# First routed rows loaded from another queue, the sigmoid table fetched earlier, and w_out's conversion one unit later

## The chip, the cores and the metric

The kernel runs on one core of a Trainium2 chip. The core has five engines with a queue of instructions each: TensorE (PE in the profile; its weight loads are PEld), VectorE (DVE), ScalarE (ACT), GpSimd (POOL) and SyncE (SP), which here only issues DMAs. Each engine works through its queue in order; semaphores hold it where it needs another's result. The metric is the device time of one execution in microseconds (us).

## The reference

Three stages follow each other: a decaying linear attention, a mixture of experts in which each token goes to one expert, and a gated dense layer. In all of them the tensors are float32.

```python
def _attn_ref(q, k, v):              # 4 batches, 8 heads, 768 steps, head dim 64
    for t in range(S):
        state = gamma * state + outer(k[:, :, t], v[:, :, t])
        y[:, :, t] = scale * q[:, :, t] @ state

def _moe_ref(x, modality_id, w_gate, modality_bias, w1, w2):   # 3072 tokens of 512, 8 experts, hidden 1024
    e_idx = np.argmax(x @ w_gate + modality_bias[modality_id], axis=1)
    for e in range(E):
        out[mask] = gate_w[mask, None] * (np.maximum(x[mask] @ w1[e], 0.0) @ w2[e])

def _moe2_ref(x, w_in, w_out):       # 512 -> 2048 -> 512, weights in float64
    h = x @ w_in
    g = h * (1.0 / (1.0 + np.exp(-1.702 * h)))
    return (g @ w_out).astype(np.float32)
```

## The kernel before

Products of float32 are computed as three matmuls of rounded halves: a value is split into a high half (`hi`, a cast on ScalarE) and a low half (`lo`, the difference, on VectorE), and hi*hi, hi*lo and lo*hi are summed in PSUM.

**Stages.** The attention writes its rows to `xd` in DRAM. The routed stage works through slots, each a block of up to 256 tokens of one expert (B), or a tiny one of 32 (T). A slot gathers its rows (`xg`, an indirect DMA that GpSimd issues), transposes them, and runs units on PE: `b1` (first layer, 24 matmuls into `psh`), `second` (second layer, into `pso`), and for a tiny slot `th`, `tt` (a transpose `ptt` that VectorE copies to `htt`), `t2` (into `psq`, from `htt` and four weight tiles) and `ts`. Results go to `ys0` and `ys1` in DRAM; `ys0` holds the first two slots, which are finished early. Weights come through `raw` tiles loaded by SyncE and split by `split` into `whi` and `wlo`; a tiny slot loads its weights straight into such tiles.

**The last routed slot** has the units `b1`, `b1`, `th`, `second`, `tt`, `b1`, `t2`, `second`, `ts`, `b1`, `second`, `second`, the tiny slot's being laid between. After each of them one entry of the list `tail` (L1049) runs: `first_loads` (the first two blocks of 128 rows for the dense stage, tiles `yg`, read from `ys0`; both lie in the one buffer `xg`), two empty entries, `first_conv(0)` (loads of the next two pieces of `w_out`), `first_turn(0)`, `first_turn(1)` (which then issues the third load, again into buffer `xg`), two empty ones, `first_turn(2)`, `first_conv(1)`. `first_turn` calls `turn`: GpSimd copies the row numbers (`idd`), PE transposes four blocks (`pyt`), ScalarE and VectorE split the result to `yh` and `yl`.

**The dense stage** handles eight tiles of 384 tokens with 16 units each. In step i, `d1` makes twelve matmuls into `psd` (three PSUM buffers), the sigmoid on ScalarE, the product `g` on VectorE, and its halves `gh` and `gl`; then `d2` of the unit two steps back (LAG = 2) makes nine matmuls into `psq`: for each of three row blocks `gh` by `woh[f]`, `gh` by `wol[f]`, `gl` by `woh[f]`. So PE's order is psd(0), psd(1), psd(2), psq(0), psd(3), psq(1) and so on.

**w_out's conversion.** The weights come as float64 and are turned to float32 halves piece by piece (class `Conv`): the constructor loads a piece (SyncE, two buffers), `A` takes its magnitude and sign (ScalarE, L956 and L957), `B` assembles the bits (VectorE, L961 to L963), `C` is a step on ScalarE (L966) and GpSimd (L967), `E` casts `woh[f]` (ScalarE, L978) and `F` makes `wol[f]` (VectorE, L981). Unit 0's halves are made in the routed stage; pieces for units 1 to 15 are made in the first tile's steps, by `more_conv`, which `d1` calls between `g` and `gh`; `A` and `B` of the piece for unit 1 have been done by `first_conv(1)`.

```python
        p0, p1, p2 = at_(i + 1), at_(i), at_(i - 1)
        for p, fs in ((p1, "C"), (p0, "A"), (p2, "E"), (p0, "B"), (p2, "F")):
            if p:
                getattr(p, fs)()
```

Here `at_(k)` is the piece for unit k + 1. Between the two stages stands a conditional block (L1076) for slots that a rare routing would need; every engine reads its condition and branches past it. The order of every queue is the order in which the code is written.

Of the kernel before, what the change touches and what calls it, by code (L numbers as in the profile page):

```python
# [8 lines left out]
F32 = mybir.dt.float32  # L9
# [3 lines left out]
AF = mybir.ActivationFunctionType  # L13
# [9 lines left out]
C = 128  # L23
# [13 lines left out]
DW = DM + 1  # L37
RP1 = NP1 * BIG
T2 = 384
NF = DFF // C  # L40
# [53 lines left out]
def tile_kernel(ctx, tc, qn, kv, mod, wg, mbias, w1, w2, w_in, w_out, c_qc, c_misc, out):  # L94
    nc = tc.nc
# [14 lines left out]
    ident = M("id")  # L110
# [14 lines left out]
    mm = {}  # L125
# [808 lines left out]
    NE = 1  # L934
# [74 lines left out]
    outv = dram_disjoint_views(out, NT)  # L1009
    yt = [pool(ctx, "yt0", 1)]  # L1010

    def yload(t, r, y=None):
        n = t * NR + r
        if y is None:
            y = yp.tile([C, DW], F32, name="yg", tag="yg")
        src, n0 = (ys0, 0) if n < RP1 // C else (ys1, RP1 // C)
        nc.sync.dma_start(y, src[(n - n0) * C:(n - n0 + 1) * C, :])
        YG[t, r] = y

    def turn(t, r, ps):  # L1020
        if r == 0:
            YT[t] = [yt[t % 2].tile([C, 4, T2], F32R, name=f"y{x}", tag=f"y{x}") for x in "hl"]
        y = YG.pop((t, r))
        n = t * NR + r
        nc.gpsimd.tensor_copy(idd[:, n:n + 1], y.bitcast(I32)[:, DM:DW])
        for k in range(4):
            nc.tensor.transpose(ps[:, k, :], y[:, k * C:(k + 1) * C], ident)  # L1027
        yh, yl = (x[:, :, r * C:(r + 1) * C] for x in YT[t])
        nc.scalar.copy(yh, ps)
        V.tensor_tensor(out=yl, in0=ps, in1=yh.bitcast(F32), op=ALU.subtract)  # L1030

    def first_loads():
        y = mm["xg"].tile([C, 2, DW], F32, name="yg", tag="xg")
        for r in range(2):
            yload(0, r, y[:, r, :])

    def first_turn(r):
        turn(0, r, mm["t"].tile([C, 4, C], F32, name="pyt", tag="pt"))
        if r == 1:
            yload(0, 2, mm["xg"].tile([C, DW], F32, name="yg", tag="xg"))  # L1040

    cq = []

# [6 lines left out]

    none = lambda: None
    tail = [first_loads, none, none, lambda: first_conv(0), lambda: first_turn(0), lambda: first_turn(1), none, none, lambda: first_turn(2), lambda: first_conv(1)]
    fin = table_final()
    for _ in range(FIN_SLOTS - 1):
# [39 lines left out]
    def d1(t, f, mid=None):  # L1094
        yh, yl = YT[t]
        ps = ps_h.tile([C, T2], F32, name="psd", tag="psd")
        m = 0
        for k in range(4):
            for a, b in ((wih, yh), (wih, yl), (wil, yh)):
                nc.tensor.matmul(ps, a[:, k, f * C:(f + 1) * C], b[:, k, :], start=(m == 0), stop=(m == 11), skip_group_check=True)  # L1100
                m += 1
        sig = gg.tile([C, T2], F32, name="sig", tag="sig")
        nc.scalar.activation(sig, ps, AF.Sigmoid, scale=1.702)  # L1103
        g = gg.tile([C, T2], F32, name="g", tag="g")
        V.tensor_tensor(out=g, in0=ps, in1=sig, op=ALU.mult)  # L1105
        if mid:
            mid()
        gh = gt.tile([C, T2], F32R, name="gh", tag="gh")
        gl = gt.tile([C, T2], F32R, name="gl", tag="gl")
        nc.scalar.copy(gh, g)  # L1110
        V.tensor_tensor(out=gl, in0=g, in1=gh.bitcast(F32), op=ALU.subtract)  # L1111
        GT[t, f] = (gh, gl)

    def d2(t, fs):
        if fs[0] == 0:
            PO[t] = [ps_o.tile([C, DM], F32, name="psq", tag=f"psq{r}") for r in range(NR)]
        for r in range(NR):
            for f in fs:
                gh, gl = GT[t, f]
                for m, (a, b) in enumerate(((gh, woh), (gh, wol), (gl, woh))):  # L1120
                    nc.tensor.matmul(PO[t][r], a[:, r * C:(r + 1) * C], b[f], start=(f == 0 and m == 0), stop=(f == NF - 1 and m == 2), skip_group_check=True)  # L1121
            if f == NF - 1:
                o = ot.tile([C, DM], F32, name="o", tag="o")
                if r % 2:
                    V.tensor_copy(o, PO[t][r])  # L1125
                else:
                    nc.scalar.copy(o, PO[t][r])  # L1127
                n = t * NR + r
                nc.gpsimd.indirect_dma_start(out=outv[n], out_offset=bass.IndirectOffsetOnAxis(ap=idd[:, n:n + 1], axis=0), in_=o, in_offset=None)  # L1129
        for f in fs:  # L1130
            del GT[t, f]
        if f == NF - 1:
            del PO[t], YT[t]
# [3 lines left out]
    def more_conv(i):  # L1137
        if len(cq) < NF - NE:
            cq.append(Conv(NF + NE + len(cq)))
        at_ = lambda k: cq[k] if 0 <= k < NF - NE else None  # L1140
# [3 lines that stand above are left out]
                getattr(p, fs)()  # L1144

    for i, (t, f) in enumerate(seq):
        d1(t, f, lambda: more_conv(i) if i <= NF - NE else None)
        if t + 1 < NT2:
            if f in (5, 6, 7):
                yload(t + 1, f - 5)  # L1150
            elif f in (11, 12, 13):
                turn(t + 1, f - 11, ps_t.tile([C, 4, C], F32, name="pyt", tag="pyt"))
        if LAG <= i < len(seq):
            t, f = seq[i - LAG]
            d2(t, [f])
# [35 lines left out]
```

## Time and profile before

| | us |
|---|---|
| median of 3 runs | 999.86 |
| lowest and highest run | 993.59, 1003.96 |
| the profiled execution | 1001.46 |
| its span, first to last instruction | 999.8 |
| PE busy in it | 965.2 |
| DVE busy | 503.1 |
| ACT busy | 410.7 |
| POOL busy | 179.1 |
| mean granted clock of TensorE | 0.992 |

The profile comes from one execution. A row of a timeline is: start in us from the span's start, duration in us, engine, line of the code, operation, tile written <- tiles read, shapes, count, and in brackets the idle time of the engine just before, with what ended it. SPq and ACTq are an engine's own sequencer, which issues DMAs and branches. A row with a count over 1 merges neighbours and spans all of them. Matmuls overlap: one that takes 0.39 us is followed 0.23 us later by the next. A row of stretches gives the stretch, its length, the busy time (and count of instructions) of PE, PEld, DVE, ACT and POOL, the granted clock of TensorE as a share of 2.4 GHz, the mean share of the DMA engines and GB/s.

### The profile page before, as it was taken

The numbers are of one execution on the slowest core, as the hardware profiler recorded it, in microseconds if no ns is written. First come the engines' busy times: TensorE is split into PE (matmuls) and PEld (weight loads), VectorE is DVE, ScalarE is ACT, GpSimd is POOL, SyncE is SP. The second block draws the span as 40 slices with busy tenths as digits, with TensorE's granted clock in tenths as the row PEclk, the third lists the DMA queues.
The fourth block names the chain that finished last, engine by engine and source line by source line (L and its number), as shares of the span: only waits on it lengthen the run. The fifth ranks groups of instructions, "written<-read, shape, count | busy, mean of one in ns | idle before, by whom it ended". The sixth has DMA issues, their size and how long they took to land.

```text
span 999.8 us, 16732 instructions
## 1 busy us (share of the span) xinstructions
PE 965.2 (97%) x6610; PEld 855.2 (86%) x6610; DVE 503.1 (50%) x921; ACT 410.7 (41%) x728; POOL 179.1 (18%) x177
## 2 busy tenths in 40 slices
PE   8999879999999999999999999999999999999995
PEld 7888668899999987879999999998999998999994
DVE  3555568798888876449942322323323223223221
ACT  3433245576777665348732222222322223222221
POOL 2343334233322222003310010010100100100101
PEclk9999999999999999999999999999999999999998
DMA  8787689888888879925310100100001001000000
GB/s 288 225 217 199 126 217 227 265 271 285 284 266 270 282 242 333 324 67 177 127 43 1 33 32 1 33 32 22 27 17 32 32 1 33 32 1 1 32 1 31
DMA packets 43128, 128.18 MB, mean 128 GB/s; under 512 B 6976, under 2 KB 7360, under 8 KB 43040
## 3 DMA queue, kind: packets, MB, share of 16 engines
q1 hardware_dynamic: 34464, 107.96, 35.0%
q0 software_dynamic: 5120, 12.77, 3.7%
q10 hardware_dynamic: 3456, 6.29, 1.9%
q8 instruction: 53, 0.87, 0.4%
q14 instruction: 35, 0.29, 0.1%
HBM read 107.76 MB, written 19.24 MB: 127 GB/s over the span
## 4 chain that ended last, share of the span: by engine, by line
PE 54%; ACT 0%; DVE 0%; POOLq 0%; POOL 0%; issue 0%; ACTq 0%
PE psq L1121 27%; PE psd L1100 26%; PE pyt L1027 1%; ACT L1103 0%; POOLq L1187 0%; DVE ab L961 0%; DVE ab L963 0%; ACT o L1127 0%; ACT ab L956 0%; ACT ab L966 0%; ACT sig L1103 0%; DVE gl L1111 0%; DVE ab L962 0%; POOL out_dram L1129 0%; POOLq L1129 0%
## 5 line engine op out<-in xcount | busy, mean ns | idle before, releaser
L1105 DVE TENSOR_TENSOR g<-psd,sig 128x384 f32<-128x384 f32 x128 | 71.3, 557 | 279.7 <-ACT sig L1103 279.7
L1103 ACT ACTIVATE sig<-psd 128x384 f32<-128x384 f32 x128 | 62.9, 492 | 289.5 <-PE psd L1100 289.5
L1100 PE MATMUL psd<-yl,wih 128*128 128x384 f32 x512 | 172.1, 336 | 0.0
L1100 PE MATMUL psd<-yh,wil 128*128 128x384 f32 x512 | 171.9, 336 | 0.0
L1100 PE MATMUL psd<-yh,wih 128*128 128x384 f32 x512 | 171.6, 335 | 0.2 <-PEq L1076 0.2
L1121 PE MATMUL psq<-woh,gh 128*128 128x512 f32 x384 | 153.9, 401 | 0.7 <-ACT gh L1110 0.7
L1121 PE MATMUL psq<-woh,gl 128*128 128x512 f32 x384 | 152.2, 396 | 1.1 <-DVE gl L1111 1.1
L1121 PE MATMUL psq<-wol,gh 128*128 128x512 f32 x384 | 152.3, 397 | 0.0
L595 DVE TENSOR_TENSOR wlo<-raw,whi 128x1024 fp32r<-128x1024 f32 x93 | 113.4, 1224 | 32.6 <-ACT whi L593 29.3
L593 ACT CAST whi<-raw 128x1024 fp32r<-128x1024 f32 x96 | 99.9, 1046 | 42.0 <-issue 16.6
L689 PE MATMUL psh<-xh,whi 128*128 128x256 f32 x384 | 109.5, 285 | 0.2 <-ACT xh L676 0.2
L689 PE MATMUL psh<-xl,whi 128*128 128x256 f32 x384 | 107.9, 281 | 0.3 <-DVE xl L677 0.3
L689 PE MATMUL psh<-xh,wlo 128*128 128x256 f32 x384 | 107.7, 281 | 0.0
L1129 POOL DMA_INDIRECT out_dram<-o,idd x24 | 23.3, 973 | 462.5 <-DVE o L1125 387.5
L1111 DVE TENSOR_TENSOR gl<-g,gh 128x384 fp32r<-128x384 f32 x128 | 71.7, 560 | 65.0 <-ACT gh L1110 65.0
L1100 PEld LDWEIGHTS psd<-yh,wih 128*128 128x128 f32 x512 | 96.5, 188 | 6.3 <-PEq L1076 0.6
L1100 PEld LDWEIGHTS psd<-yl,wih 128*128 128x128 f32 x512 | 96.0, 188 | 5.8
L1100 PEld LDWEIGHTS psd<-yh,wil 128*128 128x128 f32 x512 | 96.1, 188 | 0.0
L1110 ACT CAST gh<-g 128x384 fp32r<-128x384 f32 x128 | 65.8, 514 | 70.3 <-DVE g L1105 70.2
L1121 PEld LDWEIGHTS psq<-woh,gl 128*128 128x128 f32 x384 | 72.1, 188 | 19.0 <-DVE gl L1111 1.5
L1121 PEld LDWEIGHTS psq<-woh,gh 128*128 128x128 f32 x384 | 72.0, 188 | 13.0 <-ACT gh L1110 1.0
L1121 PEld LDWEIGHTS psq<-wol,gh 128*128 128x128 f32 x384 | 72.3, 188 | 11.6
(195 smaller groups left out, 1516.4 us busy)
## 6 DMA issues: line engine op xcount, KB each, us to landing
raw<-in_w_dram SPq DMA_DIRECT2D x96, 512.0 KB
qk<-in_qn_dram SPq DMA_DIRECT2D x23, 512.0 KB
r<-in_w_in_dram SPq DMA_DIRECT2D x16, 512.0 KB
r<-in_w_out_dram SPq DMA_DIRECT2D x16, 512.0 KB
ys<-yo SPq DMA_DIRECT2D x12, 513.0 KB
yg<-ys SPq DMA_DIRECT2D x24, 256.5 KB
v<-in_kv_dram SPq DMA_DIRECT2D x24, 256.0 KB
xd<-xr ACTq DMA_DIRECT2D x24, 256.0 KB
```

Of the source, the lines that this page charges most:

```text
L593: nc.scalar.copy(hi, raw)
L595: eng.tensor_tensor(out=lo, in0=raw, in1=hi.bitcast(F32), op=ALU.subtract)
L689: nc.tensor.matmul(ps[:, f, :], a[:, k, f * C:(f + 1) * C], b[:, k, :], start=(m == 0), stop=(m == 11), skip_group_check=True)
L1027: nc.tensor.transpose(ps[:, k, :], y[:, k * C:(k + 1) * C], ident)
L1100: nc.tensor.matmul(ps, a[:, k, f * C:(f + 1) * C], b[:, k, :], start=(m == 0), stop=(m == 11), skip_group_check=True)
L1103: nc.scalar.activation(sig, ps, AF.Sigmoid, scale=1.702)
L1105: V.tensor_tensor(out=g, in0=ps, in1=sig, op=ALU.mult)
L1110: nc.scalar.copy(gh, g)
L1111: V.tensor_tensor(out=gl, in0=g, in1=gh.bitcast(F32), op=ALU.subtract)
L1121: nc.tensor.matmul(PO[t][r], a[:, r * C:(r + 1) * C], b[f], start=(f == 0 and m == 0), stop=(f == NF - 1 and m == 2), skip_group_check=True)
L1129: nc.gpsimd.indirect_dma_start(out=outv[n], out_offset=bass.IndirectOffsetOnAxis(ap=idd[:, n:n + 1], axis=0), in_=o, in_offset=None)
```

## The change

Three edits. (1) `yload` takes the queue that issues the load; the first three loads of the dense stage's first tile are issued by GpSimd instead of SyncE. (2) `first_loads` begins with a sigmoid of one column into a scratch tile `pre`; the built program holds ScalarE's table load there and none in the dense stage. (3) `more_conv` is called with i - 1, from step 1 on instead of from step 0, and one step longer.

```diff
-    def yload(t, r, y=None):
+    def yload(t, r, y=None, eng=nc.sync):
         n = t * NR + r
         if y is None:
             y = yp.tile([C, DW], F32, name="yg", tag="yg")
         src, n0 = (ys0, 0) if n < RP1 // C else (ys1, RP1 // C)
-        nc.sync.dma_start(y, src[(n - n0) * C:(n - n0 + 1) * C, :])
+        eng.dma_start(y, src[(n - n0) * C:(n - n0 + 1) * C, :])
         YG[t, r] = y
...
     def first_loads():
+        nc.scalar.activation(mm["xg"].tile([C, 1], F32, name="pre", tag="pre"), ident[:, 0:1], AF.Sigmoid)
         y = mm["xg"].tile([C, 2, DW], F32, name="yg", tag="xg")
         for r in range(2):
-            yload(0, r, y[:, r, :])
+            yload(0, r, y[:, r, :], nc.gpsimd)
 
     def first_turn(r):
         turn(0, r, mm["t"].tile([C, 4, C], F32, name="pyt", tag="pt"))
         if r == 1:
-            yload(0, 2, mm["xg"].tile([C, DW], F32, name="yg", tag="xg"))
+            yload(0, 2, mm["xg"].tile([C, DW], F32, name="yg", tag="xg"), nc.gpsimd)
...
     for i, (t, f) in enumerate(seq):
-        d1(t, f, lambda: more_conv(i) if i <= NF - NE else None)
+        d1(t, f, lambda: more_conv(i - 1) if 0 < i <= NF - NE + 1 else None)
```

The order on GpSimd's queue in the last routed slot, first what is removed, then what is added; the row ahead is the last gather of the routed stage.

```order
 L650 DMA xg<-xd,ix 32x512
-L1025 COPY idd<-yg 128x1 x3
-L1070 TENSOR_LOAD more
-L1076 COMPARE_AND_BRANCH
+L1017 DMA yg<-ys_64 128x513 x2
+L1025 COPY idd<-yg 128x1 x2
+L1017 DMA yg<-ys_64 128x513
+L1025 COPY idd<-yg 128x1
```

The two loads stand right behind the gather, the third behind the copies that read the first two; the same three rows leave SyncE's queue, where the first two stood behind a `raw` load and ahead of the tiny slot's second weights.

ScalarE's queue in the same slot, where `hh` is the output of a `b1` unit:

```order
-L694 ACTIVATE hh<-psh 128x512 x2
+L694 ACTIVATE hh<-psh 128x512
+L1033 ACT_TABLE_LOAD
+L1033 ACTIVATE pre<-misc 128x1
+L694 ACTIVATE hh<-psh 128x512
```

The table load and the one-column sigmoid stand between the `hh` of the slot's first two `b1` units.

VectorE's queue at the head of the dense stage, before, from the end of unit 0's step on (`wol1` is the low half for unit 1):

```order
L1111 TENSOR_TENSOR gl_8555<-g_8541,gh_8554 128x384
L1105 TENSOR_TENSOR g_8573<-psd_8558,sig_8571 128x384
L961 TENSOR_SCALAR ab_8580<-ab_8580 128x512
L962 TENSOR_SCALAR ab_8580<-ab_8580 128x512
L963 SCALAR_TENSOR_TENSOR ab_8580<-r64_8543,ab_8580 128x512
L981 TENSOR_TENSOR wol1_8491<-sg_5643,woh1_8490 128x512
L1111 TENSOR_TENSOR gl_8589<-g_8573,gh_8588 128x384
```

And of the change, from the product of unit 1 on:

```order
L1106 TENSOR_TENSOR g_8564<-psd_8549,sig_8562 128x384
L961 TENSOR_SCALAR ab_8571<-ab_8571 128x512
L962 TENSOR_SCALAR ab_8571<-ab_8571 128x512
L963 SCALAR_TENSOR_TENSOR ab_8571<-r64_5516,ab_8571 128x512
L1112 TENSOR_TENSOR gl_8578<-g_8564,gh_8577 128x384
L1106 TENSOR_TENSOR g_8596<-psd_8581,sig_8594 128x384
L961 TENSOR_SCALAR ab_8603<-ab_8603 128x512
L962 TENSOR_SCALAR ab_8603<-ab_8603 128x512
L963 SCALAR_TENSOR_TENSOR ab_8603<-r64_8566,ab_8603 128x512
L981 TENSOR_TENSOR wol1_8493<-sg_5645,woh1_8492 128x512
L1112 TENSOR_TENSOR gl_8612<-g_8596,gh_8611 128x384
```

Unit 0's step now holds only `g` and `gl`; the low half `wol1` is made in the step of unit 2 instead of unit 1, and PE reads it in `psq` of unit 1, which follows psd(3) in both programs.

## Rows read from the trace of the kernel before

**Rows 1.** Busy time (share of the span) and instructions of TensorE.
```profile
PE 965.2 (97%) x6610; PEld 855.2 (86%) x6610; DVE 503.1 (50%) x921; ACT 410.7 (41%) x728; POOL 179.1 (18%) x177
```

**Rows 2.** Timeline of PE in the last two routed slots.
```profile
385.26 0.55 PE L673 MATMUL pxt<-misc,xg 128*128 128x128 f32 x3 [1.33 <-DMA xg<-xd,ix]
...
398.26 0.43 PE L661 MATMUL pxt<-misc,xg 32*128 32x32 f32 x4
...
417.42 0.38 PE L769 MATMUL ptt<-misc,ht 128*128 128x128 f32 x2
419.89 0.95 PE L1027 MATMUL pyt<-misc,yg 128*128 128x128 f32 x4 [2.09 <-DMA yg<-ys]
...
424.76 0.60 PE L1027 MATMUL pyt<-misc,yg 128*128 128x128 f32 x4
425.29 0.62 PE L778 MATMUL psq<-whi,htt 128*32 128x512 f32 x1
...
431.08 0.65 PE L1027 MATMUL pyt<-misc,yg 128*128 128x128 f32 x4
...
434.38 0.40 PE L707 MATMUL pso<-whi,hh 128*128 128x512 f32 x1
```

**Rows 3.** Stretches: busy time by engine, granted clock, DMA share and GB/s.
```profile
420.00:425.00 5.00, 5.00 (x31) 5.00 (x32) 2.16 (x3) 0.95 (x3) 1.14 (x2) 0.66 0.99 395
```

**Rows 4.** Timeline of PE in the dense stage's first tile.
```profile
447.35 0.50 PE L1121 MATMUL psq<-woh,gh 128*128 128x512 f32 x1 [0.67 <-ACT gh L1110]
...
449.17 0.51 PE L1121 MATMUL psq<-woh,gl 128*128 128x512 f32 x1 [1.08 <-DVE gl L1111]
...
453.01 0.39 PE L1121 MATMUL psq<-woh,gh 128*128 128x512 f32 x1
453.25 0.39 PE L1121 MATMUL psq<-wol,gh 128*128 128x512 f32 x1
...
482.38 0.39 PE L1121 MATMUL psq<-woh,gh 128*128 128x512 f32 x1
```

**Rows 5.** Timeline of SyncE's queue: issues of the `yg` loads.
```profile
411.63 1.17 SPq L1017 DMA_DIRECT2D yg<-ys  x2
...
425.43 0.33 SPq L1017 DMA_DIRECT2D yg<-ys  x1
```

**Rows 6.** Timeline of GpSimd: a gather, and the copies from `yg`.
```profile
377.93 0.96 POOL L650 DMA_INDIRECT xg<-xd,ix  x1 [0.30 <-issue]
...
419.90 0.18 POOL L1025 COPY idd<-yg 128x1 int32<-128x1 int32 x1 [26.70 <-DMA yg<-ys]
...
428.61 0.19 POOL L1025 COPY idd<-yg 128x1 int32<-128x1 int32 x1 [6.98 <-DMA yg<-ys]
```

**Rows 7.** Timeline of VectorE at the tiny slot's transpose.
```profile
421.50 0.42 DVE L771 COPY htt<-ptt 128x256 f32<-128x256 f32 x1
```

**Rows 8.** Timeline of ScalarE in the last routed slot.
```profile
412.79 0.60 ACT L694 ACTIVATE hh<-psh 128x512 fp32r<-128x512 f32 x1 [2.20 <-PE psh L689]
...
419.28 1.05 ACT L593 CAST whi<-raw 128x1024 fp32r<-128x1024 f32 x1 [2.24 <-DMA raw<-in_w_dram]
```

**Rows 9.** Timeline of ScalarE at the head of the dense stage.
```profile
443.49 1.28 ACT L1103 ACT_TABLE_LOAD   x1 [2.76 <-ACTq L1076]
444.79 0.49 ACT L1103 ACTIVATE sig<-psd 128x384 f32<-128x384 f32 x1
...
445.70 0.66 ACT L956 ACTIVATE ab<-r 128x512 f32<-128x512 f32 x1
...
446.80 0.50 ACT L1110 CAST gh<-g 128x384 fp32r<-128x384 f32 x1
```

**Rows 10.** Timeline of VectorE in the dense stage's first tile.
```profile
445.31 0.56 DVE L1105 TENSOR_TENSOR g<-psd,sig 128x384 f32<-128x384 f32 x1 [5.88 <-ACT sig L1103]
...
452.08 0.69 DVE L981 TENSOR_TENSOR wol<-sg,woh 128x512 fp32r<-128x512 f32 x1
...
482.22 0.68 DVE L981 TENSOR_TENSOR wol<-sg,woh 128x512 fp32r<-128x512 f32 x1
```

## The prediction

> **What bounds the kernel now.** The table of busy time comes first: TensorE (PE) is busy 965.2 us of the span of 999.8 [rows 1]. So a change can only pay where PE stands still, and I looked for PE's idle stretches beside the three edits: the timeline of PE, then of each engine that PE waits for there. There are two such places. In the last routed slot PE idles 2.09 us for the first `yg` tile [rows 2], and then runs slower: the granted clock is 0.66 of full over 420 to 425, that is partly at the lower of its two levels, 1.2 GHz [rows 3]. At the head of the dense stage PE idles 0.67 us for `gh` and 1.08 us for `gl` of the first unit [rows 4]; its matmuls keep their full speed there (0.39 us at 453.01 as at 482.38).
>
> **Edit 1, the `yg` loads on GpSimd's queue.** SyncE issued the first two at 411.63, behind weight loads [rows 5]; GpSimd copied from them at 419.90 after an idle of 26.70 us, so GpSimd's queue was free from 393.20 on [rows 6]. In the changed program they wait there only for the tile's last readers, the transposes that start at 398.26 and take 0.43 us [rows 2]. The trace has no such load from GpSimd. From below, SyncE's own third load: issued 425.43 [rows 5], copied from at 428.61 [rows 6], 3.2 us. From above, a gather that GpSimd issued at 377.93 [rows 6] and PE waited for until 385.26 [rows 2], 7.3 us. Either way the pair is there by 406 (398.7 + 7.3), 12 us before PE asks; so I count its wait as nothing, and if that cover were gone the old wait would be back. GpSimd's issues (0.96 us for the gather) lie in its idle time. On SyncE 1.17 us of issuing go away [rows 5]; the tiny slot's second weights, which stood behind the `yg` loads, come no later than before.
>
> PE then goes on where `ptt` ends: 417.42 + 0.38 = 417.80 [rows 2]. Four transposes and a `b1` unit take 3.30 us at full clock (431.08 to 434.38, [rows 2]) and the second transposes 0.53 (424.76 to 425.29), so PE is at the tiny slot's `psq` at 421.63. What is late next: `psq` reads `htt`, which VectorE copies at 421.50 to 421.92 [rows 7], queued behind the split of a weight tile that ScalarE could start only at 419.28, when `raw` landed [rows 8]. SyncE issues that `raw` ahead of the old `yg` loads, so I leave its landing where it is. `psq` starts at 421.92 + 0.05 = 421.97 instead of 425.29: **a gain of 3.32 us** (2.09 of idle, 1.57 of slow clock, less a new wait of 0.34). Bounds: 3.7 if `raw` lands 0.34 earlier; 2.0 if the pair's bytes, now sent earlier, still lie ahead of `raw` and push it back by 1.3 us (513 KB at the 395 GB/s of [rows 3]). I take 3.3, since the pair goes out 12 us earlier than before, and `raw` never stood behind it.
>
> The third `yg` load may start when the second transposes are read, about 421.7 (GpSimd has nothing else queued). With 3.2 to 7.3 us it is there between 424.9 and 429.0. PE asks 5.79 us after `psq` starts (425.29 to 431.08, [rows 2]), at 427.76: a wait of 0 to 1.2 us. A plain load is nearer to SyncE's row than to a gather, so I take 0.
> The Trainium skill ("DMA: Bandwidth & Descriptors", section on the anatomy of a DMA on the gpsimd path) fits 2.0 us plus the bytes over 436 GB/s; by it the load's 256.5 KB would take an estimated 2.6 us, and the sum would stay as it is; the gather's 7.3 us is far off that fit.
>
> **Edit 2, the table.** ScalarE's load takes 1.28 us and now stands behind a `hh` in the last routed slot, where ScalarE idles 2.20 us before the next `hh` at 412.79 [rows 8]. That hides it with the one-column sigmoid; if it did not, only a `hh` that PE reads 12 us later would be late. In the dense stage it leaves ScalarE's path: the first sigmoid can start at 443.49 instead of 444.77 [rows 9].
>
> **Edit 3, the conversion one unit behind, and where edits 2 and 3 meet.** Before, `wol` of unit 1 (the low half of `w_out`'s rows) ended at 452.08 + 0.69 = 452.77 [rows 10], and PE used it with the second matmul of `psq` 1, at 453.25 [rows 4]: just in time. The work between is a chain that no edit shortens: `A` of the next conversion (445.70, [rows 9]), its `B`, its `C`, `A` and `B` of the one after, then `F` of the first: 452.08 - 445.70 = 6.38 us. Where does `A` start now? The first sigmoid 443.49 to 443.98, `g` 444.01 to 444.57 (0.56, [rows 10]), `gh` 444.60 (0.50, [rows 9]), the second sigmoid 0.37 after it, at 444.97, and `A` 0.91 after a sigmoid starts, as before (445.70 less 444.79): 445.88. So `wol` 1 ends at 445.88 + 6.38 + 0.69 = 452.95, **0.18 later than before**, because unit 0's `g` and `gh` and the second sigmoid now stand ahead of `A`. The first unit's waits (0.67 + 1.08) vanish, but PE comes to `psq` 1 that much earlier, at 451.26, and stands there until 453.00. Against 453.25 before this gains 0.2 us; bounds 0 and 0.6 (no load, but the chain's pieces a little tighter).
> The Trainium skill ("ScalarE: Activation LUTs", section "What ACT_TABLE_LOAD costs") adds about 1.4 us of draining to the load, so the first sigmoid would come as soon as its matmuls end, and the sum would be 0.4 us better; here the row shows ScalarE's idle before the load ended by its own sequencer's branch, so no run so far shows that drain.
>
> Later in the stage the lag costs. In a step without backlog VectorE finishes `wol` at 482.22 + 0.68 = 482.90 [rows 10]. Before, that tile was used a whole unit later (4.2 us). Now it is the one that the second matmul of the `psq` at 482.38 [rows 4] reads, due at 482.62. It comes 0.3 late, with 0.05 to PE 0.34. PE is then 0.34 behind, which makes the next unit's tile punctual, and the unit after is late again: 0.34 us in every second unit, except while VectorE still lags behind and where transposes of the next tile stretch PE's unit (units 11 to 13). Carrying these durations by hand from unit to unit through the sixteen, I count four such waits: **a loss of 1.4 us** (0 if VectorE is a little quicker, 2.4 if all seven pairs pay). The loads of `w_out` on SyncE move behind one `yg` load each; they wait for their buffer until `B` has read it, so I count nothing for that.
>
> **Sum.** -3.3 - 0.2 + 1.4 = -2.1 us. The profiled execution took 1001.46 us (1.66 around its span), so it would take 999.4. The runs shown have a median 1.6 lower, 999.86, and I forecast that: **997.8 us**. Measurement cannot tell about 1% (10 us) of this kernel from no change; no case below reaches it.
>
> **Rivals.**
> - *The weights are in time after all* (the change does what it says in both places). For it: before, PE never waited on `w_out`'s halves. Against it: the 0.18 above. -3.3 - 1.75 = -5.05: 994.8 us.
> - *The clock falls at `psq` 1.* After 2.09 us without work the clock fell [rows 2, 3]; after 0.67 and 1.08 with two matmuls between it did not [rows 4]. The new wait, 1.5 to 2 us with one matmul in it, lies between. Price: the 1.57 us paid after 419.89 (5.40 us to the tiny `psq`, against 3.83). -2.1 + 1.6 = -0.5: 999.3 us.
> - *The third load takes the first one's place*, the case on the slower side. It decides once it lands 2.1 us after 427.76, 8.2 us after its issue; the gather's 7.3 comes near. At 8.5 us PE would wait 2.5 us there and again run slowly for 1.57: -2.1 + 2.5 + 1.6 = +2.0: 1001.9 us. Against it: the other queue has run dry by then.
> - *Edit 1 changes nothing*, since the moved loads wait for something else: nothing in GpSimd's queue speaks for it. The dense stage alone gives +1.2: 1001.1 us.
>
> **Chances and range.** The forecast 0.52, weights in time 0.10, clock falls 0.22, third load late 0.08, edit 1 idle 0.03, the rest unnamed. The bounds added up run from -4.3 (-3.7 - 0.6) to +3.4 (-2.0 + 2.4 + 1.2 + 1.6 for the clock): 995.6 to 1003.0; leaving out 2 in 10 at the ends, about 995.5 to 1001. Three runs of the kernel before lie between 993.59 and 1003.96, so a median of a few moves by some 2 us by itself: 993.5 to 1002.5 us. All named cases are within 1%; only the scatter of the runs gives the other two a chance: faster by over 1% 0.04, within 1% 0.93, slower by over 1% 0.03.
>
> **What would show it.** Edit 1: no wait of `pyt` on a DMA before the first transposes, the clock at full after that, and the tiny `psq` 4.6 us after `ptt` began (421.97 - 417.42) instead of 7.9 (425.29 - 417.42); a DMA wait at the third `pyt` is the third rival. Edit 2: no ACT_TABLE_LOAD in the dense stage. Edit 3: PE waits at `psq` move from `gh` and `gl` to `woh` and `wol`, about 1.5 to 2 us at unit 1, then short ones of 0.3 in odd units; no waits there means the first rival. A time below 990 or above 1010 would mean that something else moved.

## The result, and the profile after

The changed kernel takes 1005.53 us (median of ten runs, 999.01 to 1008.59); the kernel before, run beside it, 998.56 us (median of ten, 993.59 to 1003.96). The ratio is 1.0063 with a 95% interval of 1.0036 to 1.0089: slower by 6.3 us, though by less than 1%. The forecast was 997.8 us with a range of 993.5 to 1002.5; the time lies above the range and the sign is wrong. The profiled execution took 1005.32 us, with a span of 1003.7 against 999.8 before.

Busy time of the changed kernel by engine, the line that answers to [rows 1]:

```profile
PE 970.2 (97%) x6610; PEld 858.7 (86%) x6610; DVE 505.8 (50%) x921; ACT 410.0 (41%) x729; POOL 179.5 (18%) x180
```

TensorE issues the same 6610 matmuls, and they take 5.0 us longer. So it is not waiting that grew most; the matmuls themselves became slower. Where they did, I looked for last, since no edit is there. First the places that the forecast spoke of.

**The tail.** GpSimd's timeline in the changed kernel (start, duration, engine, line, operation, what it waited for), against [rows 5] and [rows 6]:

```profile
404.21 1.15 POOL L1017 DMA_DIRECT2D yg<-ys  x2 [5.56 <-PE pxt L661]
410.06 0.18 POOL L1025 COPY idd<-yg 128x1 int32<-128x1 int32 x1 [4.71 <-DMA yg<-ys]
...
427.68 0.55 POOL L1017 DMA_DIRECT2D yg<-ys  x1 [16.79 <-issue]
431.72 0.18 POOL L1025 COPY idd<-yg 128x1 int32<-128x1 int32 x1 [3.49 <-DMA yg<-ys]
```

The pair waits for the transposes that free its tile, is issued then, and is copied from 5.85 us after its issue; the third load 4.04 us after its own. Both durations lie between the forecast's bounds of 3.2 and 7.3. PE's timeline in the same slots, against [rows 2]:

```profile
423.02 0.38 PE L769 MATMUL ptt<-misc,ht 128*128 128x128 f32 x2
423.24 0.60 PE L1027 MATMUL pyt<-misc,yg 128*128 128x128 f32 x4
...
426.55 0.60 PE L1027 MATMUL pyt<-misc,yg 128*128 128x128 f32 x4
427.08 0.62 PE L778 MATMUL psq<-whi,htt 128*32 128x512 f32 x1
...
432.90 0.66 PE L1027 MATMUL pyt<-misc,yg 128*128 128x128 f32 x4
```

No `pyt` waits for a DMA any more, the first two or the third. From `ptt` to the tiny slot's `psq` it is 4.06 us, against 7.87 before [rows 2] and 4.55 in the forecast. The stretch that answers to [rows 3] runs at full clock, 1.00 in place of 0.66 (PE, PEld, DVE, ACT and POOL busy, clock, DMA share, GB/s):

```profile
423.00:428.00 5.00, 5.00 (x47) 4.21 (x49) 3.83 (x5) 2.50 (x4) 0.32 (x1) 1.00 1.02 411
```

ScalarE's timeline, against [rows 8] and [rows 9]: the table load stands behind a `hh`, the next `hh` still waits for PE and not for it, and the first sigmoid of the dense stage follows without a load. The split that VectorE's `htt` stands behind could start 0.80 us after `ptt` (423.82 - 423.02) instead of 1.86 (419.28 - 417.42), which is why even the new wait of 0.34 us that the forecast had there did not come:

```profile
415.48 0.60 ACT L694 ACTIVATE hh<-psh 128x512 fp32r<-128x512 f32 x1 [1.25 <-PE psh L689]
416.09 1.28 ACT L1033 ACT_TABLE_LOAD   x1
417.39 0.20 ACT L1033 ACTIVATE pre<-misc 128x1 f32<-128x1 f32 x1
418.35 0.60 ACT L694 ACTIVATE hh<-psh 128x512 fp32r<-128x512 f32 x1 [0.76 <-PE psh L689]
...
423.82 1.05 ACT L593 CAST whi<-raw 128x1024 fp32r<-128x1024 f32 x1 [1.21 <-DMA raw<-in_w_dram]
...
445.34 0.49 ACT L1104 ACTIVATE sig<-psd 128x384 f32<-128x384 f32 x1 [2.58 <-ACTq L1077]
```

**The dense stage.** PE's timeline in its first tile, after, against [rows 4]:

```profile
442.19 0.41 PE L1101 MATMUL psd<-yh,wih 128*128 128x384 f32 x1 [0.16 <-PEq L1077]
...
453.08 0.51 PE L1122 MATMUL psq<-woh,gh 128*128 128x512 f32 x1 [0.18 <-ACT woh L978]
454.90 0.50 PE L1122 MATMUL psq<-wol,gh 128*128 128x512 f32 x1 [1.31 <-DVE wol L981]
...
458.96 0.39 PE L1122 MATMUL psq<-woh,gh 128*128 128x512 f32 x1
...
463.74 0.50 PE L1122 MATMUL psq<-wol,gh 128*128 128x512 f32 x1 [0.18 <-DVE wol L981]
...
485.50 0.40 PE L1122 MATMUL psq<-woh,gh 128*128 128x512 f32 x1
```

and two rows of before that [rows 4] doesn't have, the stage's first matmul and the first of `psq` 2:

```profile
440.20 0.41 PE L1100 MATMUL psd<-yh,wih 128*128 128x384 f32 x1 [0.19 <-PEq L1076]
...
457.18 0.39 PE L1121 MATMUL psq<-woh,gh 128*128 128x512 f32 x1
```

The waits for `gh` and `gl` are gone, and PE stands at `psq` 1 for `woh` and `wol` instead. From the stage's first matmul to `psq` 2 it is 16.77 us (458.96 - 442.19) against 16.98 before (457.18 - 440.20): the head gains 0.21 us between these two executions. That is less than executions differ: in the seven kernels below that have the old head and keep full clock in it, the kernel before among them, this stretch takes 16.55 to 17.06 us, 16.86 in the mean. Then short waits for `wol` follow in every second unit, four in all. Only 0.14 to 0.18 us of each stands in the bracket, but the unit in which one falls takes 4.60 to 4.65 us between two `psq` in place of 4.20, and up to 0.04 more falls in the unit after it, so each costs about 0.45 us.

**Where the loss is.** PE is already late when the changed part of the program begins. The same `hh`, the 13th and the 37th of the routed stage on ScalarE, 24 units apart, in the kernel before and then in the changed one:

```profile
217.14 0.60 ACT L694 ACTIVATE hh<-psh 128x512 fp32r<-128x512 f32 x1 [0.54 <-PE psh L689]
...
355.42 0.60 ACT L694 ACTIVATE hh<-psh 128x512 fp32r<-128x512 f32 x1 [0.66 <-PE psh L689]
```

```profile
219.49 0.60 ACT L694 ACTIVATE hh<-psh 128x512 fp32r<-128x512 f32 x1 [0.73 <-PE psh L689]
...
360.73 0.60 ACT L694 ACTIVATE hh<-psh 128x512 fp32r<-128x512 f32 x1 [0.73 <-PE psh L689]
```

138.28 us become 141.24, 2.1% more, at a granted clock of 1.00 in both and without a wait of PE in between. The stretch of 24 units in the kernel before and in the changed one (length, busy time of PE, PEld, DVE, ACT and POOL, clock, DMA share, GB/s):

```profile
217.00:356.00 139.00, 139.00 (x920) 127.39 (x919) 117.14 (x145) 99.53 (x140) 42.38 (x30) 1.00 0.83 276
```

```profile
219.00:361.00 142.00, 142.00 (x921) 128.92 (x921) 117.35 (x145) 99.17 (x139) 42.36 (x30) 1.00 0.80 269
```

The loss is 0.123 us a unit. PE's timeline shows it in both kinds of block: 24 products of `b1` (`psh`), 24 of `second` (`pso`), and the next `psh`; before, and then after:

```profile
251.96 0.28 PE L689 MATMUL psh<-xh,whi 128*128 128x256 f32 x1
...
254.77 0.39 PE L707 MATMUL pso<-whi,hh 128*128 128x512 f32 x1
...
260.23 0.28 PE L689 MATMUL psh<-xh,whi 128*128 128x256 f32 x1
```

```profile
255.03 0.28 PE L689 MATMUL psh<-xh,whi 128*128 128x256 f32 x1
...
257.90 0.39 PE L707 MATMUL pso<-whi,hh 128*128 128x512 f32 x1
...
263.50 0.28 PE L689 MATMUL psh<-xh,whi 128*128 128x256 f32 x1
```

`psh` takes 2.87 us in place of 2.81, `pso` 5.60 in place of 5.46. The routed stage has 48 units; if all lose 0.123 us as these 24 do, that is 5.9 us, nearly the whole difference. For the units ahead of them, which run beside the attention, and those behind, waits and clock falls are mixed in, so their part is not shown by itself. Nothing in the code of these matmuls changed, but one thing in the diff reaches them: the early sigmoid writes into a new tile, `pre`, of the pool `xg`. Its 4 bytes a partition take 32, and in the compiled programs every tile below it moves down by 32 bytes: `xg`, `xh` (142080 to 142048) and `xl`, `hh` (123616 to 123584) and `hl`, `yo`. The weights `whi` and `wlo` stay.

### The profile page after: what moved, and what is told of

Same layout as the page of the kernel before. It is cut to its first block, busy times and chain, and to the rows that moved or that the text cites. A ratio compares the mean times of both kernels' runs of the same rounds, so it can differ in the third digit from the quotient of the medians.

```text
span 1003.7 us, 16733 instructions
## 1 busy us (share of the span) xinstructions
PE 970.2 (97%) x6610; PEld 858.7 (86%) x6610; DVE 505.8 (50%) x921; ACT 410.0 (41%) x729; POOL 179.5 (18%) x180
## 4 chain that ended last, share of the span: by engine, by line
PE 50%; DVE 2%; ACT 1%; issue 1%; POOLq 0%; POOL 0%; DVEq 0%; ACTq 0%
PE psq L1122 25%; PE psd L1101 24%; DVE ab L961 1%; PE pyt L1027 1%; DVE wol L981 1%; ACT ab L956 1%; ACT ab L966 0%; DVE ab L962 0%; DVE gl L1112 0%; POOLq L1188 0%; DVE ab L963 0%; ACT sig L1104 0%; ACT o L1128 0%; DVE g L1106 0%; ACT gh L1111 0%
## 5 line engine op out<-in xcount | busy, mean ns | idle before, releaser
L689 PE MATMUL psh<-xh,whi 128*128 128x256 f32 x384 | 111.6, 291 | 0.0
L689 PE MATMUL psh<-xl,whi 128*128 128x256 f32 x384 | 110.3, 287 | 0.1
L689 PE MATMUL psh<-xh,wlo 128*128 128x256 f32 x384 | 110.0, 286 | 0.0
```

The costliest lines, as they stand in the source:

```text
L689: nc.tensor.matmul(ps[:, f, :], a[:, k, f * C:(f + 1) * C], b[:, k, :], start=(m == 0), stop=(m == 11), skip_group_check=True)
```

## The experiments

Two theories. **Placement:** the 32 bytes slow the routed stage. **Dense:** the conversion one unit behind costs more than was counted, and the slow routed stage is scatter of one execution. The runs of one batch share their runs of the kernel before, which took about 1% longer there (1006 to 1011 us) than beside the changed kernel, so only ratios are compared. In all of them the 24-unit stretch, the blocks and the waits are read as above.

**1. The extra tile alone**, in the kernel before:

```
     def first_loads():
+        V.memset(mm["xg"].tile([C, 1], F32, name="pre", tag="pre"), 0.0)
```

> The kernel before, with one edit: a one-column tile of 4 bytes a partition more in the pool xg, set to zero by VectorE where the changed kernel runs its early sigmoid. It moves the tiles of the routed rows (xg, xh and xl, hh and hl, yo) down by 32 bytes in SBUF; nothing else differs. Theory 'placement': the changed kernel's routed stage, whose code is the same as before but whose matmuls follow each other 0.1189 us apart instead of 0.1164, is slow because of those 32 bytes; the loss there, about 5.4 us between 185 and 360, comes back here: 1004.0 us against 998.6, ratio 1.005. Theory 'dense': the loss comes from the conversion one unit behind, and the slower routed stage in the one profile is scatter between executions: 998.6 us, ratio 1.000.

Measured: ratio 1.0058 (1.0030 to 1.0086). The two `hh` in its trace are 141.24 us apart, as in the changed kernel:

```profile
224.57 0.60 ACT L694 ACTIVATE hh<-psh 128x512 fp32r<-128x512 f32 x1 [0.73 <-PE psh L689]
...
365.81 0.60 ACT L694 ACTIVATE hh<-psh 128x512 fp32r<-128x512 f32 x1 [0.73 <-PE psh L689]
```

One tile that nobody reads costs 5.8 us (3.0 to 8.6). The instruction that is added with it runs behind this stretch, in the last routed slot, so it is the tile and not the instruction that slows it.

**2. The changed kernel without the extra tile:**

```
-        nc.scalar.activation(mm["xg"].tile([C, 1], F32, name="pre", tag="pre"), ident[:, 0:1], AF.Sigmoid)
+        nc.scalar.activation(base[:, 0:1], ident[:, 0:1], AF.Sigmoid)
```

> The changed kernel, but its early sigmoid writes into the first column of an existing tile of constants that is dead by then (base), so that every tile stands where it stood before. Theory 'placement': the routed stage is as fast as before again, 1005.5 - 5.4 = 1000.1 us, ratio to before 1.0015. Theory 'dense': no change, 1005.5 us, ratio 1.007.

Measured: ratio 1.0023 (0.9995 to 1.0051), where placement said 1.0015. The two `hh` are 138.28 us apart again:

```profile
222.68 0.60 ACT L694 ACTIVATE hh<-psh 128x512 fp32r<-128x512 f32 x1 [0.55 <-PE psh L689]
...
360.96 0.60 ACT L694 ACTIVATE hh<-psh 128x512 fp32r<-128x512 f32 x1 [0.66 <-PE psh L689]
```

With run 1 this shows the cause from both sides: the tile put in, the loss is there; taken out, it is gone. All the runs here agree: in the five kernels with the tiles in their old places (before and runs 2, 4, 5, 7) the two `hh` are 138.27 to 138.28 us apart, in the three with `pre` (changed, runs 1 and 3) 141.24. Besides, this execution shows a rival of the forecast at work. After the wait at `psq` 1 the clock falls; the stretches there (columns as above):

```profile
454.29:458.29 4.00, 3.24 (x10) 2.68 (x11) 3.93 (x8) 2.68 (x5) 1.50 (x1) 0.73 0.43 133
458.29:462.29 4.00, 4.00 (x19) 3.68 (x18) 1.45 (x3) 1.44 (x3) 0.28 (x1) 0.84 0.39 131
```

From the first `psd`, at 442.29 here, to `psq` 2 at 460.65 it is 18.36 us, 1.59 more than the 16.77 of the changed kernel with nearly the same waits (0.26 and 1.32 for 0.18 and 1.31).

**3. The changed kernel with the conversion where it stood**, tile kept:

```
-        d1(t, f, lambda: more_conv(i - 1) if 0 < i <= NF - NE + 1 else None)
+        d1(t, f, lambda: more_conv(i) if i <= NF - NE else None)
```

> The changed kernel with w_out's conversion in the unit where it stood before, the two other edits and the extra tile kept. Theory 'placement' with a cheap lag (1.4 us, the term of the forecast): 1005.5 - 1.4 = 1004.1 us, ratio 1.0055. Theory 'dense': the lag costs all that was lost between 448 and the end in the two profiles, 5.3 us: 1000.2 us, ratio 1.0016.

Measured: ratio 1.0031 (1.0004 to 1.0058), between the two figures, with an interval that takes in both. The times do not settle it; its trace does better. There the lag's waits are missing: from the first `psd` to the ninth `psq` it is 41.19 us (494.12 - 452.93), against 43.31 in the changed kernel (485.50 - 442.19), so the lag costs 2.1 us up to there, 0.8 of it ahead of `psq` 2, and some 0.45 more with the fourth wait, at 508.

**4. The first two edits alone, without the tile** (both changes of runs 2 and 3):

> The kernel before with the first two edits alone: the first routed rows from GpSimd's queue and the early sigmoid, which writes into the dead tile of constants; the conversion where it stood, every tile where it stood. Theory 'placement': the gain of the tail, 3.3 us by the forecast and up to 6.9 by the two profiles (4.9 before the first sigmoid of the dense stage, 2.0 behind it), is left alone: 991.7 to 995.3 us, ratio 0.993 to 0.997. If the tail's gain is not real either: 998.6, ratio 1.000.

Measured: ratio 0.9963 (0.9933 to 0.9994), inside what was expected. This version is faster than the kernel before, though by little, and with it faster than the changed one. PE's timeline in its tail and at the head of the dense stage:

```profile
425.31 0.62 PE L778 MATMUL psq<-whi,htt 128*32 128x512 f32 x1 [1.35 <-DVE htt L771]
...
440.69 0.41 PE L1101 MATMUL psd<-yh,wih 128*128 128x384 f32 x1 [0.67 <-PEq L1077]
...
448.15 0.50 PE L1122 MATMUL psq<-woh,gl 128*128 128x512 f32 x1 [0.49 <-DVE gl L1112]
...
456.53 0.39 PE L1122 MATMUL psq<-woh,gh 128*128 128x512 f32 x1
```

Without the lag the early table gives 1.14 us at the head in this execution (15.84 to `psq` 2, against 16.98), and no wait in every second unit follows. The head varies here too: three other kernels have the same order of work in it and take 15.99 (run 3), 16.75 and 16.73 us (`e_x96_h160` and `e_x96_h192` below), so over all executions the early table is worth about 0.5 us (16.33 against 16.86 in the mean). In all four ScalarE waits there 0.99 to 1.72 us for the load of a piece of `w_out`, longest in the two slower ones. In this execution PE waits 1.35 us for `htt` in the tail, a wait of the sort that the forecast put at 0.34.

**5. The lag alone**, in the kernel before (the diff of run 3 the other way):

> The kernel before with the third edit alone, w_out's conversion one unit behind, every tile where it stood. From the traces: without the early sigmoid the chain to wol of unit 1 begins after the first unit's g and gh and about 1.3 us later than in the changed kernel, so PE passes psq 1 about 1 us later than before, and four waits of 0.45 us follow: +2.9 us, ratio 1.003. If the lag costs only what the forecast said of the steady units: +1.4 us, ratio 1.0014.

Measured: ratio 0.9995 (0.9958 to 1.0033), inconclusive: the interval holds no change, the 1.4 us and just the 2.9. The trace is clear on the place, and shows more than either figure. PE's timeline at `psq` 1 and the next stretches:

```profile
458.62 0.51 PE L1121 MATMUL psq<-woh,gh 128*128 128x512 f32 x1 [1.46 <-ACT woh L978]
460.44 0.50 PE L1121 MATMUL psq<-wol,gh 128*128 128x512 f32 x1 [1.31 <-DVE wol L981]
...
466.08 0.39 PE L1121 MATMUL psq<-woh,gh 128*128 128x512 f32 x1
```

```profile
462.00:466.00 4.00, 4.00 (x16) 3.72 (x15) 2.48 (x5) 0.50 (x2) 0.00 (x1) 0.64 0.48 173
```

From the first `psd` (446.09) it is 19.99 us to `psq` 2, 3.0 more than before, a clock fall included; with the four waits that follow, 4.8 us in all. By estimate, without the fall (1.59 us in run 2) it is 3.2, inside the interval, but only just. Why the ten timed runs of this kernel show no loss stays open.

**6. Which tiles, and what of their place.** Eight kernels that add unused space only, so that tiles move down while the code stays: in the kernel before, and in the last two on top of run 4. The edits are of one kind, here for `e_pad_h`:

```
     def first_loads():
+        V.memset(mm["h"].tile([C, 1], F32, name="pad_h", tag="pad_h", bufs=1), 0.0)
```

The expectations follow in the order of the table: `e_pad_h`,

> The kernel before with 32 bytes of unused space behind the tiles of the pool h: hh and hl (the stationary operands of the routed stage's second product, pso) and yo move down by 32 bytes, from 32 above a multiple of 64 onto a multiple of 64; x, xg and the weights stay. The first 24 products of a unit (psh) take 2.81 us in the kernel before and 2.87 in the one with all tiles moved, the 24 of pso 5.46 and 5.60. If the place of h decides pso: psh 2.81, pso 5.60, about 0.4% of the time lost (ratio 1.004). If it is x alone that matters: both as before, ratio 1.000. If being on a multiple of 64 is what is fast: pso as before or faster, ratio 1.000 or below.

`e_pad_x`,

> The kernel before with 32 unused bytes behind the tiles of the pool xt and 32 more behind those of h: xh and xl (the moving operands of psh) go down by 32, off the multiple of 64 on which they stood; hh, hl and yo go down by 64, so that they stand as before against a multiple of 64; xg stays. If only the place against multiples of 64 counts and x is the cause of psh's part: psh 2.87, pso 5.46, ratio 1.002. If it is a relation between tiles in another measure than 64: anything else, pso 5.60 among it.

`e_pad_64`,

> The kernel before with 64 unused bytes in the pool xg where the changed kernel has 32: every tile that moved in the changed kernel moves by twice as much, and stands against multiples of 64 as in the kernel before. If the place against multiples of 64 is the cause: psh 2.81, pso 5.46, ratio 1.000. If it is the distance from the weights' tiles, which stay, or any pad at all: psh and pso above those, ratio 1.003 or more.

`e_pad_96`,

> The kernel before with 96 unused bytes in the pool xg where the changed kernel has 32; one look, read by the length of PE's blocks of 24 products (psh 2.81 us, pso 5.46 before; 2.87 and 5.60 with everything 32 lower, 2.84 and 5.49 with everything 64 lower). Theory 'own place in steps of 128': a value of its own for each block, and 128 lower is as before. Theory 'distance between the two operands of a product in steps of 128' says the same of this run, and that psh and pso here equal those of the kernel whose weights are 32 and whose other tiles are 128 lower. Theory 'any pad slows': 2.84 to 2.87 and 5.49 to 5.60 for every pad.

`e_pad_128`,

> The same with 128 unused bytes. If the effect repeats in steps of 128 (either theory of place): psh 2.81, pso 5.46, as in the kernel before. If any pad slows, or the step is longer: psh 2.84 or more, pso 5.49 or more.

`e_pad_w`,

> The kernel before with 32 unused bytes behind the weights' tiles whi and wlo and 96 more in the pool xg: the weights go 32 lower, xg, x, h and yo 128 lower. If a product's time goes by the distance between its two operands in steps of 128: psh and pso as in the run with 96 unused bytes. If it goes by the own place of x in psh and of h in pso alone: 2.81 and 5.46, or, where the weights' own place counts too, both of them changed in another way than there.

`e_x96_h160`,

> The first two edits alone, with the sigmoid in the dead tile (0.996 of the kernel before), and two pads: x 96 lower, h and yo 160 lower, weights and xg in place. Theory 'distance between the operands': psh 2.755 us as in the two other runs with that distance, though xg stands elsewhere; pso at a distance not yet seen. If it is 5.46 the routed stage gains 0.055 us a unit, some 2.6 us, and the ratio is 0.994; if it is 5.60, psh's gain is lost again and the ratio is 0.998. Theory 'place of xg or yo': psh not at 2.755.

`e_x96_h192`,

> The same with h and yo 192 lower. Theory 'distance between the operands': psh 2.755 again; pso at another new distance, 5.46 to 5.60, ratio 0.994 to 0.998 by it. Theory 'place of xg or yo': psh another than in the run before.

Measured, from PE's timeline between 205 and 375 us: the mean of some 28 `psh` blocks and of the seven uninterrupted `pso` blocks of 24, by how far `x`, `h`, `xg` and the weights lie below their places in the kernel before, with the time of the 24 units between the two `hh`. The `pso` blocks of one kernel agree within 0.02 us; the `psh` blocks spread by 0.1 to 0.2, so their mean is taken and not the median of which the expectations spoke (2.755 for 96 is a median; its mean is 2.79).

| kernel | x | h | xg | weights | psh, us | pso, us | 24 units, us | ratio |
|---|---|---|---|---|---|---|---|---|
| before | 0 | 0 | 0 | 0 | 2.83 | 5.46 | 138.28 | 1 |
| run 1 | 32 | 32 | 32 | 0 | 2.89 | 5.60 | 141.24 | 1.0058 (1.0030 to 1.0086) |
| e_pad_h | 0 | 32 | 0 | 0 | 2.83 | 5.58 | 139.63 | 1.0002 (0.9967 to 1.0037) |
| e_pad_x | 32 | 64 | 0 | 0 | 2.90 | 5.50 | 140.40 | 0.9998 (0.9956 to 1.0039) |
| e_pad_64 | 64 | 64 | 64 | 0 | 2.86 | 5.49 | 139.41 | 0.9999 (0.9963 to 1.0036) |
| e_pad_96 | 96 | 96 | 96 | 0 | 2.79 | 5.60 | 138.96 | one execution |
| e_pad_128 | 128 | 128 | 128 | 0 | 2.86 | 5.58 | 140.51 | one execution |
| e_pad_w | 128 | 128 | 128 | 32 | 2.78 | 5.60 | 138.60 | one execution |
| e_x96_h160 | 96 | 160 | 0 | 0 | 2.79 | 5.61 | 138.84 | 0.9999 (0.9959 to 1.0039), run 4 in it |
| e_x96_h192 | 96 | 192 | 0 | 0 | 2.79 | 5.60 | 138.75 | 0.9966 (0.9924 to 1.0008), run 4 in it |

Single blocks as they stand in PE's timeline of `e_pad_h` (`psh` 2.81, `pso` 5.58), then a `psh` of `e_pad_96` (2.75):

```profile
239.56 0.28 PE L689 MATMUL psh<-xh,whi 128*128 128x256 f32 x1
...
242.37 0.39 PE L707 MATMUL pso<-whi,hh 128*128 128x512 f32 x1
...
247.95 0.28 PE L689 MATMUL psh<-xh,whi 128*128 128x256 f32 x1
```

```profile
256.71 0.28 PE L689 MATMUL psh<-xh,whi 128*128 128x256 f32 x1
...
259.46 0.40 PE L707 MATMUL pso<-whi,hh 128*128 128x512 f32 x1
```

What follows. The two parts come apart: moving `h` (with `yo`) slows `pso` alone, and `psh` goes with `x`. A multiple of 64 is not what matters, since 64 lower is not as before and `h` does worse on one (5.58) than off it (5.46). Nor does it repeat in steps of 128. Not every pad slows: 96 makes `psh` faster than before. `psh` is the same (2.78 to 2.79) in all four kernels in which `x` lies 96 further from the weights, whatever `xg` and `yo` do, and the one with `x` 128 and the weights 32 lower goes with these and not with `e_pad_128` (2.86). So for `psh` the distance between a product's two operands fits, and the places of `xg`, `yo` and of `x` alone don't. For `pso` the runs don't tell distance and own place apart (5.58 to 5.61 from 96 on), and neither is all: `h` and the weights lie alike in run 1 and `e_pad_h`, and `pso` takes 5.60 us in every block of the one and 5.58 in every block of the other. What in the chip makes a distance slow, and which ones, stays open. The Trainium skill ("SBUF — State Buffer", section "SBUF: two separate sides") says that PE never waits on anyone at SBUF, and gives it a second read port for the stationary operand. That is about one engine in the way of another; of a price for an operand's place it says nothing there. These runs show one: a block of 24 takes 2.78 to 2.90 us, and 5.46 to 5.61, by nothing but places. None of the tried places is better than the first for both products together: 24 units with `x` 96 lower cost 138.6 to 139.0 us against 138.28.

The timed ratios of these pads don't resolve effects of 0.4% and less; what is said of them rests on the blocks, which hardly vary. One ratio fits them badly: by its stretch `e_pad_x` loses 2.12 us in 24 units, an estimated 4.2 in 48 (ratio 1.0042), which lies just above its measured interval.

**7. The conversion one unit ahead**, on top of run 4 (the first step moves into the last routed slot, and the definition of `more_conv` moves up with it):

```
             cq[0].B()
+            more_conv(0)
...
-        d1(t, f, lambda: more_conv(i) if i <= NF - NE else None)
+        d1(t, f, lambda: more_conv(i + 1) if i < NF - NE else None)
```

> The first two edits alone, with the sigmoid in the dead tile, and w_out's conversion one unit ahead of where the kernel before has it: its first step moves into the last routed slot. If wol of unit 1 was what PE waited for at the head of the dense stage with the lag, no wait on woh or wol is left, the waits for gh and gl of unit 0 shrink to what g and gh take (0.7 us at most in all), and PE passes psq 1 0.4 to 1.1 us earlier against its first psd than without the lead; ratio 0.995 to 0.996. If the conversion's step in the last routed slot delays hh or the first sigmoid instead: a new wait of PE for ScalarE or VectorE there, ratio 0.998 or more.

Measured: ratio 1.0019 (0.9981 to 1.0057). No wait for `woh` or `wol` is left, as expected, but those for `gl` grow, and PE needs 17.54 us to `psq` 2 (460.49 - 442.95) in place of 15.84:

```profile
451.37 0.50 PE L1132 MATMUL psq<-woh,gl 128*128 128x512 f32 x1 [1.14 <-DVE gl L1122]
...
456.67 0.50 PE L1132 MATMUL psq<-woh,gl 128*128 128x512 f32 x1 [0.49 <-DVE gl L1122]
460.49 0.39 PE L1132 MATMUL psq<-woh,gh 128*128 128x512 f32 x1
```

For unit 0 the reason is VectorE: `B` and now `F` as well stand ahead of its `gl`. For unit 1 it is a load: ScalarE's timeline has `A` waiting for the next piece of `w_out`, and `gh` of unit 1 stands behind it in ScalarE's queue:

```profile
453.23 0.67 ACT L956 ACTIVATE ab<-r 128x512 f32<-128x512 f32 x1 [2.32 <-DMA r<-in_w_out_dram]
```

So at the head of the dense stage the conversion can be late or the first units can, and in these traces the place that the kernel before has is the best of the three (15.84 to 16.75 us with the early table, against 17.54 one unit ahead and 16.77 one unit behind, with the waits that follow there).

## Why the prediction was wrong

**The step that failed is edit 2's cost.** The forecast put the table load and the one-column sigmoid behind a `hh` and counted nothing more, and it took PE's rate in the routed stage for given, since no line there changed. It priced the instruction and not the tile that the instruction writes. That tile costs 5.8 us (run 1, 3.0 to 8.6), or 5.9 by the trace (48 units of 0.123). None of the forecast's rivals has it, so no chance given there covers it.

The other steps, against what was measured:

- **Edit 1, mechanism right, size too large.** The old wait is gone in all seven kernels with the edit. But 3.3 us was taken from one execution at the long end. In the nine kernels that still load from SyncE's queue, PE waits 0.62 to 2.35 us for the first `yg`, and `ptt` to the tiny `psq` takes 4.87 to 7.87 us, 6.17 in the mean; 7.87 is the one that the forecast read [rows 2]. In the seven kernels with the edit it takes 3.95 to 5.40, 4.38 in the mean. So by these means the edit is worth 1.8 us, not 3.3. The new wait for `htt` exists, 0.25 to 1.35 us in four of the seven.
- **Edit 2, the table.** Right: the load is hidden, and the first sigmoid starts without it. In the new place the load ends at 417.37 (416.09 + 1.28) and the next instruction starts at 417.39, with the `hh` ahead of it ended just as it began (415.48 + 0.60 = 416.08). The drain of about 1.4 us that the Trainium skill ("ScalarE: Activation LUTs", section "What ACT_TABLE_LOAD costs") adds to a load doesn't show there.
- **Edits 2 and 3 at the head of the dense stage.** Forecast -0.2 us, measured -0.21 (16.77 against 16.98). The chain is the forecast's: `wol` of unit 1 not earlier than before, and PE there too soon, waiting 1.49 us (0.18 + 1.31) where it had 1.74. That the size agrees to 0.01 us is luck, since the old head alone varies from 16.55 to 17.06.
- **The lag in the steady units.** Four waits, as forecast; 0.45 us each in place of 0.34, 1.8 us in place of 1.4.
- **The clock at `psq` 1.** A rival with a price of 1.6 us. It did not happen in the changed kernel's profile and did in run 2's, at 1.59 us. It fell in run 5 too, so in two of the three profiled executions with the lag. Nor was the old head safe from it, as the rival took from its one row: in `e_pad_w`, behind unit 0's waits of 0.75 and 1.07 us, the clock was 0.78 and 0.79 over 457 to 465, and the way to `psq` 2 took 18.64 us. It is a matter of the execution.
- **The third load late.** Did not happen; it was copied from 4.04 us after its issue, well ahead of the 8.2 that would have decided. The 2.6 us estimated from the Trainium skill's fit ("DMA: Bandwidth & Descriptors", section on the anatomy of a DMA on the gpsimd path) is 1.4 short of that row, in which the DMA engines were at a share of 0.58.

Summed anew: placement +5.9, edit 1 -1.8, head of the dense stage -0.2 (or +1.4 where the clock falls), steady units +1.8: +5.7 us, or +7.3. Measured +6.3, within 3.6 to 8.9. Without the tile the same sum is -0.2 or +1.4; run 2 has +2.3, interval -0.5 to +5.1. Without the lag as well it is -1.8 - 1.1 = -2.9, or -2.3 with the 0.5 of the mean head; run 4 has -3.7, interval -6.7 to -0.6.

One sum of the forecast is off by itself: its upper bounds, -2.0 + 2.4 + 1.2 + 1.6, make +3.2 and not +3.4. The 1003.0 us given with it goes with +3.2. Neither reaches the +6.3 measured.

## What to carry to other kernels

Read a diff for the memory that it allocates as well as for its instructions: a new tile in a pool moves the tiles of others, so compare the addresses of the two compiled programs before costing an edit at nothing, and put a scratch result into space that exists already. When a profile is slower, line up the same instruction in both traces from the start; where a drift grows evenly and no code changed, as here, look at the clock and at the places of the tiles before the edit's own waits. A wait that comes from one execution is a sample, so read it in several runs before taking its removal as the gain.

## What the hardware showed that was not expected

- Matmuls of the same shape, at the same granted clock and with no wait, differ by up to 4% in pace with the places of their operands in SBUF (`psh` 2.78 to 2.90 us, `pso` 5.46 to 5.61 a block of 24), in steps as small as 32 bytes, and alike in every execution: 24 units take 138.27 to 138.28 us in five kernels with one layout, 141.24 in three with another.
- A pause of PE of about 1.5 us with one matmul in it lowered the clock in one execution (0.73, then 0.84 over 454 to 462 in run 2) and not in another with nearly the same waits (the changed kernel).
- The load of two `yg` tiles made PE wait anything from 0.62 to 2.35 us in nine executions of kernels that issue it alike.
